# A state-space and MLP block on one core: the last four token tiles get a PSUM tile each, and the last is multiplied in two column halves

## The chip, the cores and the metric

The kernel runs on one core of a Trainium2 chip. The metric is the device time of one execution in microseconds (us), here as the median of a few runs. A profile is one execution recorded by the hardware profiler; its span goes from the first instruction to the last.

## The reference

A layer with two residual halves over 2048 tokens of width 512: a state-space convolution (S4), then an MLP. Layer norms go ahead of each; the MLP has a second one inside.

```python
def _B_ref(x, w1, b1, w2, b2):
    y = _layernorm(x, axis=-1)
    h = _gelu(jnp.einsum("bsd,df->bsf", y, w1) + b1)      # 512 -> 1376
    return jnp.einsum("bsf,fd->bsd", h, w2) + b2          # 1376 -> 512

x = A_u                                                    # (1, 2048, 512), bfloat16
h = x + _A_ref(_layernorm(x, axis=-1), ...)                # S4: y = irfft(rfft(u) * rfft(K)) + u * Dskip
h2 = h + _B_ref(_layernorm(h, axis=-1), B_w1, B_b1, B_w2, B_b2)
return h2
```

The change lies in the last product, `h @ w2`, its residual add and its stores.

## The kernel before

The whole kernel is written as a list of operations. `add(engine, cost, fn, r=, w=, new=)` puts one operation on the list with what it reads and writes; an estimated cost goes with it. `S.run` then plays the list through on a model of the engines and gives each engine its order: at every step the engine that could start first takes the ready operation with the lowest rank. The program is issued in that order, so a change of a cost or of a dependency can move instructions.

PSUM is cut into four slots of 128 x 1024 float32 values (`NSL = 4`). An object `Ps()` stands for one use of a slot; it takes a free slot at the operation that names it in `new`, and gives it back when all operations that read or write it are planned. Dependencies on PSUM are kept for the whole `Ps` object, not for its columns: an operation that writes any part of it comes after every earlier operation that reads any part. If the model sees TensorE without work for over 0.6 us, it puts in filler matmuls (`fill`, L1451) on a free slot.

The tokens are worked in four groups of 512: `mlp(0, 0)`, `mlp(0, 1)`, `mlp(1, 0)` and `mlp(1, 1)`, the last of them at the very end of the kernel. Each call makes, for 512 tokens:

- the first product, 11 slices of 128 hidden values (the last has 97 rows, 96 and a row of ones for the bias), 4 matmuls of 512 columns for each (L1341), and ScalarE's Gelu out of PSUM into `hT` (L1343);
- the second product, in two rounds (`jp`) of two token tiles (`z`) of 128 tokens. One `Ps` holds both tiles of a round, 512 columns each. A tile takes 11 matmuls of 128 x 512 (L1358), one for each slice of `hT` with its own weight load, in three operations of 4, 4 and 3;
- the residual add on VectorE (L1360), which reads the tile's 512 columns in PSUM and the residual in SBUF and writes a bfloat16 buffer `ot` (eight of these in turn);
- two stores of 64 rows x 512 columns, 64 KB each (L584), both issued by SyncE (`dma("SP", ...)`).

So the second tile of a round writes to a `Ps` that the first tile's add reads: its first matmul waits for that add. In the last call the order on TensorE is: tile 1 (11 matmuls), 4 matmuls of tile 3, tile 2 (11), the other 7 of tile 3, 3 filler matmuls, tile 4 (11). At the end of the program SyncE waits for every store and the engines meet at a barrier (L1491).

`not_[0]` counts the token tiles as they are listed, 1 to 16, four for each call.

Of the kernel before, what the change touches and what calls it, by code (L numbers as in the profile page):

```python
# [9 lines left out]
ACT = mybir.ActivationFunctionType  # L10
ALU = mybir.AluOpType
# [234 lines left out]
class Sched:  # L246
# [10 lines left out]
    def add(self, eng, cost, fn, r=(), w=(), new=(), lat=0.0, pr=None, byts=0, soft=(), softw=(), hv=None):  # L257
        o = Op()
        o.soft = sorted({self.wr[k] for x in soft for k in self.keys(x) if k in self.wr} | {i for x in softw for k in self.keys(x) for i in self.rd.get(k, ())})
        o.eng = eng if isinstance(eng, tuple) else (eng,)  # L260
        o.cost = cost if isinstance(cost, tuple) else (cost,)
        o.fn, o.lat, o.i, o.new, o.byts = fn, lat, len(self.ops), tuple(new), byts
        o.ni, o.act = 0, 0.0
        o.hv = int(o.eng[0] == "DVE") if hv is None else hv
        o.pr = self.pr if pr is None else pr
        o.key = "%g%s" % (o.pr, o.eng[0][0])
        o.pr = RANK.get(o.key, o.pr)
        deps = set()
        for x in r:
            for k in self.keys(x):  # L270
                p = self.wr.get(k)
                if p is not None:
                    deps.add(p)
        for x in w:
            for k in self.keys(x):
                p = self.wr.get(k)
                if p is not None:
                    deps.add(p)
                deps.update(self.rd.get(k, ()))
        for x in r:  # L280
            for k in self.keys(x):
                self.rd.setdefault(k, []).append(o.i)
        for x in w:
            for k in self.keys(x):
                self.wr[k] = o.i
                self.rd[k] = []
        o.deps = sorted(deps)
        o.ps = [x for x in list(r) + list(w) if isinstance(x, Ps)]
        self.ops.append(o)
        return o  # L290
# [143 lines left out]
def c_act(n, ptr=0):  # L434
    return 0.055 + n / 1200.0 + 0.09 * min(ptr, 1)


def c_dve(n, mode=1, psum=False):
    return (0.09 if n < 64 else 0.065) + (0.07 if psum and n > 700 else 0) + n / mode / 960.0
# [3 lines left out]
def kernel(ctx, tc, A_u, A_A_re, A_A_im, A_B_re, A_B_im, A_C_re, A_C_im, A_log_dt, A_Dskip,  # L443
           B_x, B_w1, B_b1, B_w2, B_b2, out):
    nc = tc.nc
    act, dve, gp = nc.scalar, nc.vector, nc.gpsimd
# [15 lines left out]
    pe = Pe()  # L462
# [9 lines left out]
    add = S.add  # L472

    def pst(p, dt=f32):
        a = slots[p.slot][:]
        return a if dt == f32 else a.bitcast(dt)
# [7 lines left out]
    def at(lo, dt, *shape):  # L484
        return V(ar, lo, dt, shape)
# [96 lines left out]
    def dma(q, out_fn, in_fn, byts, r, w, pr=None, soft=(), k=1.0):  # L582
        eng = {"SP": nc.sync, "ACT": nc.scalar, "POOL": nc.gpsimd}[q]
        add(q, 1.0 if q == "POOL" else 0.55, lambda e: eng.dma_start(out_fn(), in_fn()), r=r, w=w, byts=byts * k, pr=pr, soft=soft)  # L584
# [174 lines left out]
    def tr(nm):  # L759
        p = Ps()  # L760

        def fn(e):
            for d in range(4):
                pe.transpose(pst(p, bf16)[:, 128 * d:128 * d + 128], raw[nm].ap()[:, d, :], identb.ap())
        add("PE", 0.6, fn, r=[raw[nm], identb], w=[p], new=[p])
        return p, (lambda: nat(pst(p, bf16)[:, 0:512]))
# [3 lines left out]
    p, pa = tr("are")  # L770
# [22 lines left out]
    p = Ps()  # L793
# [41 lines left out]
    p, pa = tr("aim")  # L835
# [385 lines left out]
    NFC = 11  # L1221
    fsz = [P] * 10 + [97]
# [7 lines left out]
    hT = at(Kg[0].lo, bf16, NFC, 512)  # L1230
    w1s = [at(EA2.lo + 2752 * c, bf16, F) for c in range(4)]
    w2s = [at(IA2.lo + 1024 * fc, bf16, 512) for fc in range(11)]
# [3 lines left out]
    ov = out_dram.rearrange("(b q h j) d -> b h j q d", b=2, j=8, h=2)  # L1236
# [90 lines left out]
    not_ = [0]  # L1327

    def mlp(b, sb, ybuf, pr):
        S.pr = pr  # L1330
        for f0 in range(0, NFC, 2):
            p = Ps()
            for z in range(2):
                fc = f0 + z
                if fc >= NFC:
                    continue
                fs = min(P, F - fc * P)

                def fn(e, p=p, z=z, fc=fc, fs=fs):
                    for dc in range(4):  # L1340
                        pe.matmul(pst(p)[:fs, 512 * z:512 * z + 512], lhsT=w1s[dc].ap()[:, fc * P:fc * P + fs], rhs=ybuf.ap().rearrange("p (t c) k -> p c t k", c=4)[:, dc], start=(dc == 0), stop=(dc == 3))  # L1341
                add("PE", 0.87, fn, r=[ybuf] + w1s, w=[p], new=[p] if z == 0 else [])
                add("ACT", c_act(512, 1), lambda e, p=p, z=z, fc=fc, fs=fs: act.activation(hT.ap()[:fs, fc, :], pst(p)[:fs, 512 * z:512 * z + 512], ACT.Gelu_apprx_tanh, bias=b1_sb.ap()[:fs, fc:fc + 1], scale=1.0),  # L1343
                    r=[p, b1_sb, TBL], w=[hT[fc]])
        for jp in range(2):
            p = Ps()
            for z in range(2):
                t = 2 * jp + z
                j = 4 * sb + t
                hh = hs[8 * b + j]  # L1350
                ot = ots[not_[0] % 8]
                not_[0] += 1

                for part in ((0, 4), (4, 8), (8, 11)):
                    def fn(e, p=p, z=z, t=t, part=part):
                        for fc in range(*part):
                            fs = fsz[fc]
                            pe.matmul(pst(p)[:, 512 * z:512 * z + 512], lhsT=hT.ap()[:fs, fc, 128 * t:128 * t + 128], rhs=w2s[fc].ap()[:fs], start=(fc == 0), stop=(fc == NFC - 1))  # L1358
                    add("PE", 0.217 * (part[1] - part[0]), fn, r=[hT[part[0]:part[1]]] + w2s[part[0]:part[1]], w=[p], new=[p] if z == 0 and part[0] == 0 else [])
                add("DVE", c_dve(512, 1, True), lambda e, p=p, z=z, hh=hh, ot=ot: dve.tensor_tensor(ot.ap(), pst(p)[:, 512 * z:512 * z + 512], hh.ap(), ALU.add), r=[p, hh], w=[ot])  # L1360
                for h in range(2):
                    dma("SP", lambda j=j, h=h: ov[b, h, j], lambda ot=ot, h=h: ot.ap()[64 * h:64 * h + 64], 65536, [ot], [("out", b, j, h)])

# [61 lines left out]
    tail(0, 0, y2T[0], 30)  # L1427
    tail(0, 1, y2T[1], 31)
    mlp(0, 0, y2T[0], 70)
    xspec(1, Two(XB), 18.8, q_="SP")  # L1430
    for c in range(NCH):
        inverse(1, c, [(KFb[0][c], XBc[c]), (KFb[1][c], XR[c])], ZT1[c], 52 + 3 * c)
    load_x(1, 65)
    mlp(0, 1, y2T[1], 71)
    tail(1, 0, y2T[2], 66)
    tail(1, 1, y2T[0], 67)
    mlp(1, 0, y2T[2], 73)
    mlp(1, 1, y2T[0], 74)

# [56 lines left out]
```

## Time and profile before

| | |
|---|---|
| median of 3 runs (lowest, highest) | 271.92 us (271.52, 274.41) |
| the profiled execution, whole | 270.04 us |
| its span | 268.3 us |
| granted TensorE clock | 1.00 |
| TensorE busy | 233.6 us, 87% |
| VectorE busy | 186.6 us, 70% |
| ScalarE busy | 169.2 us, 63% |
| L1358, second product, 128 x 512 | 172 recorded matmuls, 380 ns each |
| L1360, residual add | 16, 691 ns each |
| stores of the output | 32 of 64 KB, 2.0 us from issue to landing |

In the profile's rows a line such as L1358 is a line of the kernel's file, `ps` is PSUM and `ar` the one large SBUF buffer in which all tiles lie. PE is TensorE, PEld its weight loads, DVE VectorE, ACT ScalarE and SP SyncE; a `q` behind the name means the engine's instruction queue, where DMAs are issued. Matmuls overlap: each lasts some 0.38 us by the record, while the next starts about 0.21 us after it.

### The profile page before, as it was taken

The page shows a single profiled execution, that of the slowest core. Times are in us where ns is not written, and L with a number is a line of the kernel's source. Part 1 is how long each engine was busy: PE and PEld are TensorE (multiplying, and loading weights), DVE is VectorE, ACT ScalarE, POOL GpSimd, SP SyncE. Part 2 cuts the span into 40 slices and gives each one's busy share as a digit, 9 for nine tenths or more (in the row PEclk, how much of TensorE's full clock was granted, in tenths as well). Part 3 has the DMA queues.
Part 4 walks back from the last instruction along what each step waited for, and adds up shares of the span by engine and source line. Part 5 has one row for each costly group of instructions (what it writes and reads, how often), then busy time and mean ns, then how long its engine had stood idle before and what let it go on. Part 6 is the DMA issues. An engine that isn't in the chain of part 4 may idle for free.

```text
span 268.3 us, 7345 instructions
## 1 busy us (share of the span) xinstructions
PE 233.6 (87%) x3038; PEld 132.4 (49%) x3058; DVE 186.6 (70%) x366; ACT 169.2 (63%) x202; POOL 59.3 (22%) x237
## 2 busy tenths in 40 slices
PE   7128788686889999999989999799999999999993
PEld 3015553343477656673667776454444444444441
DVE  3899999999999897576965986798447249031031
ACT  3798989898988598868962773457405504704700
POOL 8999923699600000000000000000000000000000
PEclk9999999999999999999999999999999999999999
DMA  6800100270755377979999999913411402411011
GB/s 139 312 1 1 42 20 20 64 216 0 169 149 161 101 220 246 363 220 306 299 288 270 235 231 204 212 24 57 78 42 39 78 20 59 81 32 47 0 33 48
DMA packets 45843, 34.36 MB, mean 128 GB/s; under 512 B 26129, under 2 KB 42226, under 8 KB 45810
## 3 DMA queue, kind: packets, MB, share of 16 engines
q1 hardware_dynamic: 45378, 33.50, 48.4%
q8 instruction: 24, 0.39, 0.6%
q10 hardware_dynamic: 432, 0.39, 0.5%
q14 instruction: 9, 0.07, 0.1%
HBM read 16.32 MB, written 10.49 MB: 100 GB/s over the span
## 4 chain that ended last, share of the span: by engine, by line
PE 61%; DVE 18%; ACT 6%; POOL 6%; issue 4%; DMA 2%; SPq 1%; DVEq 0%; ACTq 0%; POOLq 0%
PE ps L1358 14%; PE ps L1341 14%; PE ps L1209 7%; PE ps L971 4%; PE ps L1451 4%; ACT ar L572 4%; PE ps L1159 3%; PE ps L1046 3%; DVE ar L923 3%; DVE ar L634 2%; POOL ar L620 2%; ACT ar L1052 2%; PE ps L1287 2%; DMA AU_d<-ar 2%; PE ps L1125 2%
## 5 line engine op out<-in xcount | busy, mean ns | idle before, releaser
L572 ACT CAST ar<-ps 128x1024 bf16<-128x1024 f32 (+3 forms) x68 | 61.0, 938 | 28.8 <-PE ps L1209 17.3
L1343 ACT ACTIVATE ar<-ps,ar 128x512 bf16<-128x512 f32 (+1 forms) x44 | 29.8, 685 | 41.4 <-PE ps L1341 28.8
L574 DVE CAST ar<-ps 128x1024 bf16<-128x1024 f32 (+2 forms) x32 | 37.3, 1181 | 8.9 <-PE ps L971 3.4
L620 POOL TENSOR_SCALAR ar<-ar 128x128 bf16<-128x128 bf16 (+6 forms) x60 | 38.1, 656 | 6.8 <-ACT ar L641 6.6
L1358 PE MATMUL ps<-ar 128*128 128x512 bf16 (+1 forms) x172 | 39.1, 380 | 0.6 <-DVE ar L1360 0.4
L1341 PE MATMUL ps<-ar 128*128 128x512 bf16 (+1 forms) x176 | 38.6, 379 | 0.1
L1360 DVE TENSOR_TENSOR ar<-ps,ar 128x512 bf16<-128x512 f32 x16 | 11.1, 691 | 38.0 <-PE ps L1358 27.6
L1052 ACT ACTIVATE ar<-ps 128x1024 bf16<-128x1024 int16 x36 | 35.3, 1037 | 1.9 <-PE ps L1046 1.4
L1199 DVE TENSOR_TENSOR ar<-ar 128x1024 bf16<-128x1024 bf16 x48 | 30.1, 686 | 8.0 <-PE ps L1209 7.8
L1358 PEld LDWEIGHTS <-ar 128*128 128x128 bf16 (+1 forms) x176 | 16.8, 97 | 22.5 <-issue 3.1
L1341 PEld LDWEIGHTS <-ar 128*128 128x128 bf16 (+1 forms) x176 | 17.6, 100 | 20.7 <-issue 0.4
L1209 PE MATMUL ps<-ar 64*128 64x128 bf16 x768 | 23.7, 217 | 2.6 <-DVE ar L1295 1.4
L1046 PE MATMUL ps<-ar 128*32 128x256 f16 x560 | 22.2, 275 | 3.9 <-ACT ar L1052 2.7
L1209 PEld LDWEIGHTS <-ar 64*128 64x128 bf16 x768 | 21.6, 94 | 7.2 <-issue 5.0
L1451 PE MATMUL ps<-ar 128*128 128x512 bf16 (+1 forms) x77 | 20.7, 387 | 0.6 <-ACT ar L572 0.2
L1046 PEld LDWEIGHTS <-ar 128*32 128x32 f16 x560 | 13.6, 97 | 13.9 <-issue 13.7
L971 PE MATMUL ps<-ar 128*64 128x512 bf16 (+1 forms) x160 | 17.6, 342 | 0.6 <-ACT ar L572 0.3
L784 ACT ACTIVATE ar<-ar 128x1024 bf16<-128x1024 f32 x16 | 15.8, 1043 | 2.2 <-DVE ar L618 2.2
L1294 DVE TENSOR_TENSOR ar<-ps,ar 128x512 bf16<-128x512 f32 x12 | 7.8, 685 | 11.7 <-ACT ar L1343 11.1
L641 ACT ACTIVATE ar<-ar 128x512 f32<-128x512 f32 (+8 forms) x18 | 11.6, 675 | 5.5 <-DMA ar<-in_A_log_dt_dram 2.1
L1426 POOL MEMSET ar<- 1x512 bf16 x1 | 0.5, 519 | 65.1 <-DVE ar L574 65.1
L1072 DVE TENSOR_TENSOR ar<-ar 128x1024 bf16<-128x1024 bf16 x21 | 14.6, 713 | 0.4 <-ACT ar L1052 0.4
(99 smaller groups left out, 322.6 us busy)
## 6 DMA issues: line engine op xcount, KB each, us to landing
AU_d<-ar SPq DMA_DIRECT2D x16, 256.0 KB, 4.9
ar<-AU_d SPq DMA_DIRECT2D x8, 512.0 KB, 6.7
ar<-AK_d SPq DMA_DIRECT2D x8, 512.0 KB, 5.5
ar<-in_A_u_dram SPq DMA_DIRECT2D x4, 512.0 KB, 6.8
AK_d<-ar SPq DMA_DIRECT2D x2, 1024.0 KB, 6.5
ar<-in_A_u_dram SPq DMA_DIRECT2D x8, 256.0 KB, 7.7
AK_d<-ar SPq DMA_DIRECT2D x4, 512.0 KB, 7.9
out_dram<-ar SPq DMA_DIRECT2D x32, 64.0 KB, 2.0
```

Source lines behind the costliest of these rows:

```text
L572: act.copy(out_fn(), in_fn())
L574: dve.tensor_copy(out_fn(), in_fn())
L620: en.tensor_scalar(a, b, f(s1), f(s2), op0, op1)
L971: pe.matmul(pst(p)[64 * h:64 * h + 64, w * (k + r):w * (k + r) + w], lhsT=T.ap()[:, f, r, :], rhs=v[f:f + 1].ap()[:, 0, :], start=True, st ...
L1046: pe.matmul(pst(p)[32 * g:32 * g + 32, 256 * j:256 * j + 256], lhsT=W2[DELTAS.index(d)].ap(), rhs=S2[g].ap()[:, ch0:ch0 + 256], start=Fals ...
L1052: add("ACT", c_act(1024), lambda e, p=p, sc=sc, cs=cs: act.activation(swo(sc[cs]) if hf and kind == "B" else sc[cs].ap().rearrange("p a b ...
L1199: dve.tensor_tensor(o, a, b_[:, :, ::-1, :] if sw else b_, ALU.mult)
L1209: pe.matmul(pst(p)[:, 512 * h + 128 * k:512 * h + 128 * k + 128], lhsT=q.ap()[rows, 2 * k + r, :], rhs=TP[w].ap()[rows, f0 // 2 + k, :], s ...
L1341: pe.matmul(pst(p)[:fs, 512 * z:512 * z + 512], lhsT=w1s[dc].ap()[:, fc * P:fc * P + fs], rhs=ybuf.ap().rearrange("p (t c) k -> p c t k", ...
L1343: add("ACT", c_act(512, 1), lambda e, p=p, z=z, fc=fc, fs=fs: act.activation(hT.ap()[:fs, fc, :], pst(p)[:fs, 512 * z:512 * z + 512], ACT. ...
L1358: pe.matmul(pst(p)[:, 512 * z:512 * z + 512], lhsT=hT.ap()[:fs, fc, 128 * t:128 * t + 128], rhs=w2s[fc].ap()[:fs], start=(fc == 0), stop=( ...
L1451: pe.matmul(slots[z][:, 0:512], lhsT=w, rhs=x, start=True, stop=True)
```

## The change

The tiles 13 to 16, the four of the last call, are marked with `fin`. Each of them gets a `Ps` of its own. The last tile is made in two halves of 256 columns, each with its own `Ps`, 11 matmuls, an add and two stores of 64 rows x 256 columns; of these, the stores of the lower 64 rows go through ScalarE's queue. The cost of a matmul in the list is now by column (0.000424 x 512 = 0.217, as before). For the first twelve tiles the operations are the same.

```diff
-                for part in ((0, 4), (4, 8), (8, 11)):
-                    def fn(e, p=p, z=z, t=t, part=part):
-                        ...
-                            pe.matmul(pst(p)[:, 512 * z:512 * z + 512], ..., rhs=w2s[fc].ap()[:fs], ...)
-                    add("PE", 0.217 * (part[1] - part[0]), fn, ..., w=[p], new=[p] if z == 0 and part[0] == 0 else [])
-                add("DVE", c_dve(512, 1, True), ... dve.tensor_tensor(ot.ap(), pst(p)[:, 512 * z:512 * z + 512], hh.ap(), ALU.add), r=[p, hh], w=[ot])
-                for h in range(2):
-                    dma("SP", lambda j=j, h=h: ov[b, h, j], ... ot.ap()[64 * h:64 * h + 64], 65536, [ot], [("out", b, j, h)])
+                fin = not_[0] > 12
+                cols = ((0, 256), (256, 512)) if not_[0] == 16 else ((0, 512),)
+                for c0, c1 in cols:
+                    if fin and z + c0 > 0:
+                        p = Ps()
+                    for part in ((0, 4), (4, 8), (8, 11)):
+                        def fn(e, p=p, z=z, t=t, part=part, c0=c0, c1=c1):
+                            ...
+                                pe.matmul(pst(p)[:, 512 * z + c0:512 * z + c1], ..., rhs=w2s[fc].ap()[:fs, c0:c1], ...)
+                        add("PE", 0.000424 * (c1 - c0) * (part[1] - part[0]), fn, ..., w=[p], new=[p] if part[0] == 0 and (fin or z == 0) else [])
+                    add("DVE", c_dve(c1 - c0, 1, True), ... dve.tensor_tensor(ot.ap()[:, c0:c1], pst(p)[:, 512 * z + c0:512 * z + c1], hh.ap()[:, c0:c1], ALU.add), r=[p, hh], w=[ot[c0:c1]])
+                    for h in range(2):
+                        dma("ACT" if h and len(cols) == 2 else "SP", lambda ...: ov[b, h, j][:, c0:c1], ... ot.ap()[64 * h:64 * h + 64, c0:c1], 128 * (c1 - c0), [ot[c0:c1]], [("out", b, j, h, c0)])
```

More of the change, by code (lines that the diff above doesn't have):

```diff
@@ L1352, in mlp @@
                 not_[0] += 1
-                for part in ((0, 4), (4, 8), (8, 11)):
-                    def fn(e, p=p, z=z, t=t, part=part):
[L1356 to L1360, printed above, removed]
-                for h in range(2):
-                    dma("SP", lambda j=j, h=h: ov[b, h, j], lambda ot=ot, h=h: ot.ap()[64 * h:64 * h + 64], 65536, [ot], [("out", b, j, h)])
+                fin = not_[0] > 12
[5 more added lines that the diff above has]
+                        def fn(e, p=p, z=z, t=t, part=part, c0=c0, c1=c1):
+                            for fc in range(*part):
+                                fs = fsz[fc]
+                                pe.matmul(pst(p)[:, 512 * z + c0:512 * z + c1], lhsT=hT.ap()[:fs, fc, 128 * t:128 * t + 128], rhs=w2s[fc].ap()[:fs, c0:c1], start=(fc == 0), stop=(fc == NFC - 1))
+                        add("PE", 0.000424 * (c1 - c0) * (part[1] - part[0]), fn, r=[hT[part[0]:part[1]]] + w2s[part[0]:part[1]], w=[p], new=[p] if part[0] == 0 and (fin or z == 0) else [])
+                    add("DVE", c_dve(c1 - c0, 1, True), lambda e, p=p, z=z, hh=hh, ot=ot, c0=c0, c1=c1: dve.tensor_tensor(ot.ap()[:, c0:c1], pst(p)[:, 512 * z + c0:512 * z + c1], hh.ap()[:, c0:c1], ALU.add), r=[p, hh], w=[ot[c0:c1]])
+                    for h in range(2):
+                        dma("ACT" if h and len(cols) == 2 else "SP", lambda j=j, h=h, c0=c0, c1=c1: ov[b, h, j][:, c0:c1], lambda ot=ot, h=h, c0=c0, c1=c1: ot.ap()[64 * h:64 * h + 64, c0:c1], 128 * (c1 - c0), [ot[c0:c1]], [("out", b, j, h, c0)])
     S.pr = 8
```

## The prediction

> **What bounds the kernel now.** I read the page first, for the span and the stores, then the chain of work that ended last over the final 30 us, then the timeline of the last 10 us, and last the rows that give prices for shapes which the end does not have yet. The core works at a granted clock of 1.00 throughout, and the change touches only what is issued after 253.28 us, so only the end needs to be read.
>
> The chain of work that ended last, in order of time (start, length, what):
>
> ```profile
> 253.28 7.23 PE ps L1358 x32
> 260.51 0.04 DVEq L1360
> 260.55 0.04 issue
> 260.59 0.70 DVE ar L1360
> 261.29 0.04 issue
> 261.33 2.55 PE ps L1358 x11
> 263.88 0.02 issue
> 263.91 0.69 DVE ar L1360
> ```
>
> TensorE multiplies three of the last four tiles in one run (33 matmuls, one without a record) and ends at 260.51. Then it waits: the VectorE add of the third tile, 0.70 us, stands between it and the fourth tile's 11 matmuls, because both tiles share one PSUM tile and the kernel's list of dependencies knows only the whole tile. The fourth tile ends at 263.88, its add at 264.60. The timeline shows what TensorE does in the gap, and what follows the last add:
>
> ```profile
> 260.33 0.81 PE L1451 MATMUL ps<-ar 128*128 128x512 bf16 x3
> ...
> 264.63 1.10 SPq L584 DMA_DIRECT2D out_dram<-ar  x2
> ```
>
> The three L1451 matmuls are filler that keeps the clock up; their first start, 260.33, is where the fourth tile could have started. After the last add SyncE issues two stores one behind the other (1.10 us together; the second starts at 265.1). The list of SyncE's waits and the view of the output tensor give the rest:
>
> ```profile
> SPq L1491 <- DMA out_dram<-ar: 1.5, 1, 1.5
> ...
> DMA to landing us min/median/max: 1.9/2.0/3.5
> ```
>
> A store lands about 2.0 us after its issue, so the second one lands near 267.2, where the 1.5 us wait of the program's end (from 265.8) ends too. 1.1 us of closing semaphores follow, to 268.3. So the last 8 us are one serial chain: wait for an add, 11 matmuls, an add, two issues, a landing, the close.
>
> **The change, part by part.** The instruction order of the changed kernel is the same as before up to the eighth matmul row of the second tile; nothing earlier moves on any engine.
>
> *Own PSUM tiles.* The four tiles go to four different slots, the fourth's second half to a fifth, which is the first tile's slot again. Before, two matmuls of L1358 waited for VectorE: the second tile's first (hidden behind four matmuls of the third) and the fourth's. Now only the very last group waits, for the first tile's add, which ends at 255.70 + 0.69 = 256.39, some 5 us earlier. The three slots that are newly entered were last read by ScalarE, whose last reading ends at 253.33 + 0.69 = 254.02. So TensorE runs on without a stop, the filler is gone, and the fourth tile starts at 260.33 in place of 261.33.
>
> *Two column halves.* 11 matmuls of 512 columns become 22 of 256, with 22 weight loads in place of 11. The end of the kernel has no such matmul, but its beginning has, with weights of the same 128x128:
>
> ```profile
> 24.60 1.04 PE L1004 MATMUL ps<-ar 128*128 128x256 f16 x8
> ...
> L1004 PEld LDWEIGHTS <-ar x80: 95/98/153, 21.9 to 39.2; 128*128 128x128 f16 x80
> L1004 PE MATMUL ps<-ar x80: 268/273/422, 22.3 to 39.3; 128*128 128x256 f16 x80
> ```
>
> Eight take 1.04 us, of which the last one's own duration is 0.273, so one follows the other after (1.04 - 0.273) / 7 = 0.110 us, and the weight load of 0.098 lies beside it. 22 of them take 21 x 0.110 + 0.273 = 2.58 us, against 2.55 for the 11 wide ones. TensorE therefore ends at 260.33 + 2.58 = 262.91 in place of 263.88: 0.97 us gained, all of it from the lost wait. The bound on the other side is that the loads are not hidden at all (22 x 0.097 = 2.13 us more); I take the row, since it is the same shape.
>
> *Half an add at the end.* The first half's add runs while TensorE does the second half: it can start near 261.7 and is over by 262.2, ahead of the last at 262.94. For the price of 256 columns out of PSUM I have another line's pair of shapes beside the add's own row:
>
> ```profile
> L1360 DVE TENSOR_TENSOR ar<-ps,ar 128x512 bf16<-128x512 f32 x16 | 11.1, 691 | 38.0 <-PE ps L1358 27.6 <-issue 7.7 <-DMA out_dram<-ar 2.6
> ...
> L629 DVE TENSOR_TENSOR ar<-ps,ar 128x512 f32<-128x512 bf16 x4 | 2.5, 682 | 0.0
> ...
> L629 DVE TENSOR_TENSOR ar<-ps,ar 128x256 f32<-128x256 bf16 x2 | 0.8, 420 | 3.5 <-PE ps L764 3.5
> ```
>
> Half the columns cost 682 - 420 = 262 ns less, so the last add takes 691 - 262 = 429 ns and 0.26 us is gained. The add ends at 262.94 + 0.43 = 263.37.
>
> *Stores.* Two stores of 64 KB become four of 32 KB; the first pair is issued from about 262.25 and SyncE is free again by 262.8 or so (it is busy with the third tile's stores from 261.3 to 262.4), before the last pair at 263.40. ScalarE has nothing else to do after 254.02, so nothing queues behind its two issues. The last pair is now issued side by side by SyncE and ScalarE, so the second issue at 264.63 + 0.5 is no longer behind the first: up to 0.5 us. What two queues do to each other is seen only in the first microseconds, in loads:
>
> ```profile
> 1.66 0.42 ACTq L584 DMA_DIRECT2D ar<-in_A_B_re_dram  x1
> 1.67 0.44 SPq L584 DMA_DIRECT2D ar<-in_A_C_im_dram  x1
> ...
> ar<-in_A_B_re_dram ACTq DMA_DIRECT2D x1, 128.0 KB, 4.1
> ...
> ar<-in_A_C_im_dram SPq DMA_DIRECT2D x1, 128.0 KB, 4.3
> ```
>
> Issued 0.01 us apart, neither issue longer than alone, they land 0.2 us apart. So of the 0.5 I count 0.3, with bounds of 0 (the pair costs as much as one behind the other) and 0.6 (half the bytes also land a little sooner). The last landing is then near 263.40 + 2.0 + 0.2 = 265.6 in place of 267.2.
>
> The Trainium skill speaks against this part: DMA: Bandwidth & Descriptors, section Rules for kernel authors, says of two transfers to disjoint partition halves not to bother, since both spread over the same 16 DMA engines and serialise whichever engine issued them; its section on issuing engines grants two queues only the issue time. The 0.2 us between the landings of the two loads above agrees with the shared engines; by that rule the gain of this part is the 0.3 taken here, not 0.5. A stricter rule is a rival below.
>
> **Sum.** 0.97 + 0.26 + 0.3 = 1.53 us, every term on the one chain, and the closing 1.1 us unchanged. The profiled execution takes 270.04 us, its span 268.3 and 1.7 around it; the changed one should show a span near 266.8 and 268.5 in all. The three runs shown have their median at 271.92, 1.9 above the profiled one; taking the same 1.53 from the median gives 270.4, or 0.6% less.
>
> **Rivals.**
> 1. *The second queue saves nothing.* The pair's second store starts its work only when the first is through with its issue, as it does now on one queue. Then the stores give 0 and the gain is 1.23: 270.7. For it: now each issue takes about 0.5 and the second store lands that much later. Against it: the loads at 1.66 and 1.67. Perfetto Trace Analysis, section DMA Instruction — HWDGE, in the Trainium skill says that the descriptor block is shared by the issuing sequencers and locked for exclusive use, which would do just this; the side-by-side issues of 0.42 and 0.44 us do not show a lock of such length.
> 2. *Weight loads come out from behind the narrow matmuls* (the other side). A load of 0.097 us beside a matmul step of 0.110 leaves 0.013 to spare; if each pair runs one after the other, the last tile takes 22 x 0.097 = 2.13 us more than I count, and the result is 271.92 - 1.53 + 2.13 = 272.5. It decides for slower from a step of 0.110 + 1.53 / 22 = 0.18 us. Against it: L1004 does the same at 0.110.
> 3. *A late last store.* One store of the first of the last four tiles took 3.5 us to land where the others took 2.0. If the last one, on a queue unused since the first 2 us, comes out like that, 1.5 of the 1.53 is lost: 271.9. Against it: that landing lies next to an instruction fetch near 257.5, and ScalarE's first loads, on a queue just as unused, land like SyncE's.
> 4. *The change does not lift the wait*, because a slot is still held or filler stays in. Then only 0.26 + 0.3 remains: 271.4. The issue order excludes nearly all of it: the last group's wait is for an add that is long done.
>
> **How the numbers follow.** The forecast has 0.76, the rivals 0.1, 0.05, 0.06 and 0.03. The likeliest time is 270.4. The mechanism alone gives 270.1 (0.6 for the stores) to 270.7. A time as measured also carries the runs' own scatter: the three of before lie from 271.52 to 274.41, and the profiled one at 270.04, so a median of a few can stand 1 us off in either direction. The range goes from 269.1 (forecast, 1.3 low) to 271.9 (rivals 3 and 4, or the forecast 1.5 high). About 1% is what a measurement of this kernel can tell from no change, 2.7 us, and no row allows a gain of that size: the bounds add up to 0.97 + 0.26 + 0.6 = 1.83. Faster by over 1% is thus the forecast and scatter together, a quarter; slower by over 1% needs rival 2 or 3 and scatter, 0.05; the rest, 0.70, lies within 1%.
>
> **What would show it.** Right: the chain near its end reads L1358 without a VectorE piece between matmuls from 253.28 to about 262.9; no L1451 after 241.0 us; two adds of 0.43 us, the last starting near 262.94; SyncE and ScalarE issues within 0.05 us of each other near 263.4; a span near 266.8. Wrong in the first step: a VectorE piece still between L1358's groups. Wrong in the second: 22 narrow matmuls that take much over 2.6 us. Wrong in the third: last landing more than 2.4 us after its issue. Wrong altogether: a difference that begins before 253 us.

## The result and the profile after

The changed kernel takes 268.80 us (median of 6 runs, 268.11 to 270.64) against 271.72 for the kernel before (median of 6, 271.25 to 274.41): ratio 0.9886, 95% interval 0.9838 to 0.9935. Two more comparisons of the same two kernels, with 12 runs of the changed one in each, gave 0.9953 (0.9926 to 0.9981) and 0.9930 (0.9890 to 0.9970), at medians of 269.85 and 270.00 us. The medians are over all runs; the ratios leave out runs that lie over 1.5% above the fastest of their kernel. All three intervals lie below 1, so the changed kernel is faster, by about 0.6%; the first figure of 1.1% did not come back. The forecast of 270.4 us stands near the two later medians, and its range of 269.1 to 271.9 misses the first one by 0.3.

The profiled execution of the changed kernel has a span of 268.9 us, 0.6 longer than the one shown of before, so spans must not be compared here. The end of the kernel can be. The chain of work that ended last, in order of time (start, length, what), reads now:

```profile
245.97 9.50 PE ps L1341 x44
255.47 9.56 PE ps L1363 x55
265.02 0.02 issue
265.05 0.42 DVE ar L1365
```

There is no VectorE piece between the matmuls any more: all 55 of the last four tiles (33 wide and 22 narrow) are one run. The groups by form in the last 14 us (count | busy us, mean ns of one | idle before):

```profile
L1363 PEld LDWEIGHTS <-ar 128*128 128x128 bf16 x50 | 4.9, 98 | 4.0
L1363 PE MATMUL ps<-ar 128*128 128x256 bf16 x20 | 2.5, 272 | 0.0
...
L1365 DVE TENSOR_TENSOR ar<-ps,ar 128x256 bf16<-128x256 f32 x2 | 0.8, 424 | 1.2 <-PE ps L1363 1.2
```

The narrow matmuls are as L1004's were, without idle time, and the half add takes 424 ns. The timeline of the last microseconds, then the DMA view with the size and the time from issue to landing:

```profile
263.41 2.55 SPq L584 DMA_DIRECT2D out_dram<-ar  x4
...
264.36 1.65 ACTq L584 DMA_DIRECT2D out_dram<-ar  x2
```

```profile
out_dram<-ar ACTq DMA_DIRECT2D x2, 32.0 KB, 2.1
out_dram<-ar SPq DMA_DIRECT2D x2, 32.0 KB, 2.0
```

The last pair, in the timeline from 265.2 us on:

```profile
265.50 0.47 SPq L584 DMA_DIRECT2D out_dram<-ar  x1
265.50 0.50 ACTq L584 DMA_DIRECT2D out_dram<-ar  x1
```

It is issued side by side, at 265.50 by both engines. The two stores land 2.08 us (SyncE) and 2.26 us (ScalarE) later; in the kernel before, the first of the last pair took 1.92.

To set kernels side by side I count from the first add of the last four tiles, ahead of which the kernel before and the changed one issue the same instructions in the same order. The stretch from there to the end of the span is called the tail below; the first expectations count theirs from the first recorded matmul of the last product instead, 2.4 to 2.6 us earlier. All times in us from the first add, two profiles of the kernel before, three of the changed one, one of each other kernel:

| kernel | TensorE ends | last add ends | last store lands | span ends |
|---|---|---|---|---|
| before (two profiles) | 8.17 | 8.90 | 11.48, 11.49 | 12.57, 12.56 |
| changed | 7.07 | 7.54 | 9.74 to 9.82 | 10.85 to 10.92 |
| own tiles alone | 7.04 | 7.77 | 10.36 | 11.43 |
| own tiles, two queues | 7.04 | 7.77 | 10.00 | 11.02 |
| own tiles, halves, one queue | 7.07 | 7.54 | 10.44 | 11.48 |
| halves and two queues, shared tile | 8.88 | 9.34 | 11.46 | 12.56 |

The end is shorter by 12.57 - 10.92 = 1.65 to 12.56 - 10.85 = 1.71 us, 0.6% of 271. It repeats within 0.1 us, while the first add stands anywhere from 255.41 to 259.68 us in the nine profiles of the table. Most of the gain comes from the own tiles: they alone bring 1.14 us of the tail (12.57 to 11.43), the second queue 0.41 more (11.02), and the halves the last 0.10 to 0.17.

### The profile page after: what moved, and what is told of

The parts are those of the page before. It is cut to its first block, busy times and chain, and to the rows that moved or that the text cites. A ratio compares the mean times of both kernels' runs of the same rounds, so it can differ in the third digit from the quotient of the medians.

```text
span 268.9 us, 7389 instructions
## 1 busy us (share of the span) xinstructions
PE 236.0 (88%) x3066; PEld 133.6 (50%) x3066; DVE 186.8 (69%) x367; ACT 169.2 (63%) x202; POOL 58.4 (22%) x237
## 4 chain that ended last, share of the span: by engine, by line
PE 49%; DVE 18%; DMA 14%; POOL 6%; ACT 6%; issue 4%; SPq 2%; DVEq 0%; ACTq 0%; POOLq 0%
PE ps L1363 14%; PE ps L1341 14%; DMA AK_d<-ar 6%; DMA ar<-in_B_w_dram 4%; ACT ar L572 3%; DVE ar L923 3%; PE ps L1046 3%; PE ps L971 3%; DVE ar L634 2%; POOL ar L620 2%; ACT ar L1052 2%; DMA AU_d<-ar 2%; PE ps L1125 2%; PE ps L1287 2%; SPq L584 2%
## 5 line engine op out<-in xcount | busy, mean ns | idle before, releaser
L574 DVE CAST ar<-ps 128x1024 bf16<-128x1024 f32 (+2 forms) x32 | 37.3, 1181 | 10.7 <-PE ps L971 4.5
L1363 PE MATMUL ps<-ar 128*128 128x512 bf16 (+3 forms) x187 | 39.4, 367 | 0.2 <-DVE ar L1365 0.2
L620 POOL TENSOR_SCALAR ar<-ar 128x128 bf16<-128x128 bf16 (+6 forms) x60 | 37.3, 643 | 6.8 <-ACT ar L641 6.6
L1341 PE MATMUL ps<-ar 128*128 128x512 bf16 (+1 forms) x176 | 38.6, 379 | 0.1
L1365 DVE TENSOR_TENSOR ar<-ps,ar 128x512 bf16<-128x512 f32 (+1 forms) x17 | 11.2, 660 | 36.4 <-PE ps L1363 28.7
L1363 PEld LDWEIGHTS <-ar 128*128 128x128 bf16 (+1 forms) x187 | 17.9, 98 | 21.2 <-issue 2.4
L1341 PEld LDWEIGHTS <-ar 128*128 128x128 bf16 (+1 forms) x176 | 17.6, 100 | 20.6 <-issue 0.4
L1456 PE MATMUL ps<-ar 128*128 128x512 bf16 (+1 forms) x83 | 20.4, 386 | 0.0
L1294 DVE TENSOR_TENSOR ar<-ps,ar 128x512 bf16<-128x512 f32 x12 | 7.8, 683 | 11.7 <-ACT ar L1343 11.1
```

The lines of the kernel that those rows point to most:

```text
L574: dve.tensor_copy(out_fn(), in_fn())
L620: en.tensor_scalar(a, b, f(s1), f(s2), op0, op1)
L1363: pe.matmul(pst(p)[:, 512 * z + c0:512 * z + c1], lhsT=hT.ap()[:fs, fc, 128 * t:128 * t + 128], rhs=w2s[fc].ap()[:fs, c0:c1], start=(fc == ...
L1456: pe.matmul(slots[z][:, 0:512], lhsT=w, rhs=x, start=True, stop=True)
```

## The experiments

Two theories were set against each other. By the tail theory the change is worth what the end of the trace shows and no more. By the whole-kernel theory it also speeds up something ahead, which would make up the 2.9 us of the first comparison.

**The two kernels once more.** No edit.

> The kernel before against itself, to see the scatter. Both theories expect a ratio of 1.000, with an interval that shows how far a ratio can stray by chance. Tail theory (the change is worth only what its traces show after the first L1358 matmul of the last round, 15.0 us before and 13.4 after): the stretch ahead of that matmul, 253.3 us in the first profile, comes out different by 1 us or more here, and the tail again 15.0 within 0.1. Whole-kernel theory (the change also speeds up something ahead of the tail, by another 1.3 us): the stretch ahead of the tail stays at the upper end, near 254.5 to 255.5.

Measured: ratio 1.0013 (0.9976 to 1.0051), 12 runs from 269.43 to 275.9 us. The tail is 12.56 (14.98 as the expectation counts it); the first add stands at 257.55 where the first profile had it at 255.70.

> The changed kernel once more. Tail theory: tail 13.4 us again, the time 1.6 us (0.6%) under the kernel before, ratio 0.994, the first comparison's 0.9886 having been scatter of the stretch ahead. Whole-kernel theory: ratio 0.989 again, 2.9 us.

Measured: ratio 0.9953 (0.9926 to 0.9981), tail 10.85.

> The changed kernel a third time, since its first two comparisons gave 0.9886 and 0.9953. Tail theory (1.65 to 1.72 us of 271, all of it after the first add of the last four tiles): a ratio near 0.994, with a profile whose stretch ahead of that add is the kernel before's, 255.4 to 257.9 us, as the run has it. Whole-kernel theory: 0.989.

Measured: ratio 0.9930 (0.9890 to 0.9970), tail 10.86, first add at 257.81. What follows: the tail theory holds as far as these runs can tell. 0.994, the tail's share, lies inside both repeats' intervals and just outside the first comparison's (0.9935 at most); 0.989 lies outside the first repeat's and just on the edge of the second's. The prediction named a difference that begins before 253 us as the sign of being altogether wrong. There is one: the first add stands at 257.81 to 257.94 in the three profiles of the changed kernel, 2.1 to 2.2 us later than in the first profile of the kernel before. But the kernel before, run again, has it at 257.55, and the kernel with own tiles alone at 255.41, so this difference comes and goes without the change. It also arises early: from the third call's first add to the last call's it is 20.14 us in all nine profiles of the table.

Where the scatter ahead of the tail comes from is partly to be seen. The busy time of the engines PE, PEld, DVE, ACT and POOL (GpSimd) from 48 to 52 us, in the first profile of the kernel before and then in that of the same kernel run again (the figure behind POOL's is the granted clock, then the DMA share and GB/s):

```profile
48.00:52.00 4.00, 3.05 (x40) 1.34 (x39) 3.90 (x8) 3.20 (x5) 2.58 (x5) 1.00 0.13 29
```

```profile
48.00:52.00 4.00, 3.69 (x24) 1.17 (x23) 3.90 (x8) 2.85 (x5) 2.60 (x5) 0.61 0.08 20
```

In some executions the clock falls to half for 3.4 us here, in others not, with the same instructions, and in the changed kernel too (0.60 in its first profile). In the second of these profiles ScalarE's work is 0.33 us late after it. That is not all: the third profile of the changed kernel has the full clock throughout and is 2 us behind the first profile of the kernel before all the same, from about 157 us on. There the list of waits from 130 to 180 us has lines that the first profile of the kernel before does not have in that stretch:

```profile
PEld L971 <- DMA ar<-AK_d: 1.5, 2, 1.0
...
PE ps L971 <- DMA ar<-AK_d: 1.0, 2, 0.8
```

TensorE waits for loads, in a stretch where the DMA engines are busy nearly all the time. The second profile of the kernel before has both waits too, 0.7 and 0.5 us, and is 1.83 us late from 157 us on, so they come without the change too. Why these loads come later in one execution than in another is not shown.

**Own tiles alone.**

```diff
-                cols = ((0, 256), (256, 512)) if not_[0] == 16 else ((0, 512),)
+                cols = ((0, 512),)
```

> Only the own PSUM tiles: each of the last four tiles has a use of PSUM of its own, the last is multiplied whole, and all stores go by SyncE. Tail theory: TensorE runs through, the tail is 15.0 - 0.97 = 14.0 us, two stores issued one behind the other at the end, ratio 0.996. Whole-kernel theory: if the unexplained part comes with the own tiles, ratio near 0.992 with a tail of 14.0.

Measured: ratio 0.9957 (0.9931 to 0.9983), tail 11.43 from the first add, 13.85 from the first recorded matmul: 1.14 us less than before where 0.97 was expected, or 1.00 without the 0.03 for narrow matmuls, which this kernel does not have. The chain of this kernel shows where the other 0.14 come from:

```profile
252.99 9.47 PE ps L1363 x43
262.46 0.02 issue
262.48 0.69 DVE ar L1365
```

With (9.47 - 0.38) / 42 the step is 0.216 us. In the kernel before, the run of 32 recorded matmuls takes (7.23 - 0.38) / 31 = 0.221: its 31 steps hold 0.14 us too much. In the trace that is one step of 0.35 between two matmuls, where the second tile waits for the first tile's add. I had called this wait hidden behind four matmuls of the third tile; they cover all but 0.14 us of it.

**Own tiles and halves, one queue.**

```diff
-                        dma("ACT" if h and len(cols) == 2 else "SP", ...)
+                        dma("SP", ...)
```

> The whole change but for the queue: own tiles and column halves, all stores by SyncE. Tail theory: last add 0.26 us shorter than in the kernel with own tiles alone, the last store's issue 0.5 us behind the one before it, so a tail of 13.4 + 0.3 = 13.7 us, between 13.4 (a second queue is worth nothing) and 14.0 (worth all of the issue time); ratio 0.995. Whole-kernel theory: if the second queue brings the unexplained part, the ratio is at 0.995 here while the full change stays at 0.989.

Measured: ratio 1.0001 (0.9968 to 1.0034), tail 11.48 from the first add. Counted as the expectation counts it, from the first recorded matmul, it is 13.9 against 13.85 with own tiles alone, so the expected 13.7 was missed: next to the whole change (10.85 to 10.92) the second queue is worth 0.56 to 0.63 us here, twice the 0.3 that was counted. The ratio was missed too: its interval leaves out the expected 0.995 and does not show the 1.1 us that the trace shows gained, though the medians do in part (270.05 against 270.85). Whether scatter of the size just shown is all of that, one profile cannot tell. The tail alone says that halving brings nothing without the second queue, and the timeline shows what eats the shorter add:

```profile
261.12 3.66 SPq L584 DMA_DIRECT2D out_dram<-ar  x6
261.61 0.42 DVE L1365 TENSOR_TENSOR ar<-ps,ar 128x256 bf16<-128x256 f32 x1 [0.52 <-PE ps L1363]
262.76 0.42 DVE L1365 TENSOR_TENSOR ar<-ps,ar 128x256 bf16<-128x256 f32 x1 [0.72 <-PE ps L1363]
```

SyncE issues six stores without a stop, 0.6 us each. The last add ends at 263.18, but the first store of the last half is issued only at 263.60, 0.42 after it, and the second 0.60 later. The add ends 0.23 us earlier than in the kernel with own tiles alone, the last landing is 0.08 later.

**Own tiles and the second queue, whole last tile.**

```diff
-                cols = ((0, 256), (256, 512)) if not_[0] == 16 else ((0, 512),)
+                cols = ((0, 512),)
...
-                        dma("ACT" if h and len(cols) == 2 else "SP", ...)
+                        dma("ACT" if h and not_[0] == 16 else "SP", ...)
```

> Own PSUM tiles, the last tile multiplied and added whole, its two 64 KB stores issued by SyncE and ScalarE side by side. Read from the end of the trace, counted from the first add of the last four tiles to the end of the span (12.57 us in the kernel before, 11.43 with own tiles alone, 10.85 to 10.92 with the whole change). Tail theory: the second queue takes 0.3 us off the own tiles, 11.1 us. If the second queue is worth nothing without the halves: 11.4. If it is worth all of the 0.5 us between two issues: 10.9.

Measured: tail 11.02, 0.41 less than own tiles alone (ratio 0.9934, 0.9885 to 0.9982), so between the expected 11.1 and the 10.9 of a queue that is worth all of the issue time. The timeline has both issues at the same moment, and the DMA view has the landings:

```profile
264.44 0.47 SPq L584 DMA_DIRECT2D out_dram<-ar  x1
264.45 0.55 ACTq L584 DMA_DIRECT2D out_dram<-ar  x1
```

```profile
out_dram<-ar SPq DMA_DIRECT2D x1, 64.0 KB, 1.9
out_dram<-ar ACTq DMA_DIRECT2D x1, 64.0 KB, 2.2
```

To 0.01 us, the stores land 1.93 (SyncE) and 2.20 us (ScalarE) after their issues, where one queue had them 1.92 and 2.04 after issues 0.52 apart. The second issue comes 0.51 us sooner after the add; of this, 0.16 comes back as a later landing, and 0.35 is gained there. The rest of the 0.41 lies in the close.

**Halves and two queues without own tiles.**

```diff
-                fin = not_[0] > 12
+                fin = False
...
-                        add("PE", ..., new=[p] if part[0] == 0 and (fin or z == 0) else [])
+                        add("PE", ..., new=[p] if part[0] == 0 and z == 0 and c0 == 0 else [])
```

> Column halves of the last tile and the second queue, but PSUM as in the kernel before: two token tiles share one PSUM tile, and so do the two halves. Tail theory: the waits stay, and a second one comes in, as the second half's first matmul waits for the first half's add: drain 0.17, add 0.43 and 0.06 of signalling, 0.66 us. The last add is 0.27 us shorter and the stores 0.3 us: 12.57 + 0.66 - 0.57 + 0.04 for narrow matmuls = 12.7 us from the first add to the end, no better than before. If the halves and the queue are worth something by themselves, it is 12.0.

Measured: tail 12.56, the same as the kernel before; ratio 1.0003 (0.9976 to 1.0030). Its chain has two waits:

```profile
264.53 0.04 issue
264.57 0.70 DVE ar L1365
265.28 0.04 issue
265.32 1.38 PE ps L1363 x11
266.70 0.02 issue
266.72 0.44 DVE ar L1365
267.16 0.04 issue
267.20 1.38 PE ps L1363 x11
```

The second half starts 0.50 us after the first has ended, so TensorE ends 0.71 us later than in the kernel before (8.88 against 8.17). What shorter add and second queue bring (0.73 against 0.46 us for the add, then 2.58 against 2.12 to the landing) is just eaten. The parts of the change do not add up. On own tiles the halves cost 0.05 us with one queue (11.43 to 11.48) and bring 0.10 to 0.17 with two; without own tiles, halves and second queue together bring nothing. The second queue alone on shared tiles was not run.

**Further the same way.** Own tiles for the last eight token tiles, with the halves and queues as in the change:

```diff
-                fin = not_[0] > 12
+                fin = not_[0] > 8
```

> The whole change, with own PSUM tiles for the last eight token tiles in place of four (the last two of the four calls). Tail theory: the wait of 0.82 us that the chain shows at 240.5 us in the kernel before goes too, with the 0.16 us that the second tile waits; the end is as in the changed kernel (10.85 to 10.92 from the first add), and from the last call's first L1341 matmul nothing else changes. 1.0 to 1.1 us under the changed kernel, ratio to the kernel before 0.991. Rival: the call's next product waits for something else (its layer norm, transposes), and nothing is gained over the changed kernel, 0.995.

Measured: 267.85 us, the lowest median of all kernels here, and ratio 0.9888 (0.9855 to 0.9921). This interval overlaps two of the changed kernel's three, so the trace has to show the gain. The tail is 10.82, as in the changed kernel, and the chain has nothing but TensorE over the last two calls:

```profile
224.31 9.50 PE ps L1341 x44
233.81 9.51 PE ps L1363 x44
243.32 9.50 PE ps L1341 x44
252.82 9.56 PE ps L1363 x55
```

In the kernel before, the chain through the third call's second product was

```profile
233.09 0.05 issue
...
240.45 0.70 DVE ar L1360
...
243.73 1.30 PE ps L1341 x6
```

It took from 233.09 (the first matmul has no record) to the next L1341 at 243.73, 10.64 us; now it takes 9.51. The third call's first add stood 20.14 us ahead of the last call's, now 19.01. Both ways 1.13 us are gained, as much as in the last call, where 1.0 to 1.1 was expected.

> The whole change, with own PSUM tiles for all sixteen token tiles. In the first two calls of the kernel before the chain shows no VectorE piece between L1358's matmuls: TensorE has 8 matmuls of L1287 to do between the third and the fourth tile, which cover the wait. Tail theory: nothing more to gain than with eight, ratio 0.990, and perhaps a loss, as PSUM's four slots are now taken by single tiles where other work wants them. Rival: each call gains the 1.1 us that the third and the fourth gained, two more: 0.981.

The edit is `fin = True`. Measured: ratio 0.9894 (0.9860 to 0.9928), no more than with eight. In the kernel before, the chain through the second call's products was

```profile
211.89 0.99 PE ps L1287 x8
...
213.25 6.87 PE ps L1358 x31
220.12 0.99 PE ps L1287 x8
221.11 2.48 PE ps L1358 x11
223.59 9.50 PE ps L1341 x44
```

and with sixteen own tiles it is

```profile
212.98 0.99 PE ps L1287 x8
213.97 9.62 PE ps L1363 x44
223.58 1.85 PE ps L1287 x16
225.44 1.40 PE ps L1456 x6
226.84 9.50 PE ps L1341 x44
```

L1287's matmuls stood where the wait would have been, and covered it. With own tiles the second eight of each call no longer stand there: sixteen of them come behind the second call's 44, and then six filler matmuls (L1456), 1.40 us, which the kernel before does not have there. The next L1341 follows the filler without a gap, so the trace does not show how early it could have started, nor what the planner saw missing. From the first call's L1341 to the third's it takes 226.84 - 183.22 = 43.62 us in place of 223.59 - 181.04 = 42.55, so 1.07 are lost in the first two calls, and the 1.13 of the third are taken back. The ratio is too coarse to show this loss. The same wait that costs 1.1 us in the last two calls costs nothing where TensorE has other work.

**A smaller last piece.** With eight own tiles, the last tile split into 384 and 128 columns.

```diff
-                cols = ((0, 256), (256, 512)) if not_[0] == 16 else ((0, 512),)
+                cols = ((0, 384), (384, 512)) if not_[0] == 16 else ((0, 512),)
```

> As the kernel with eight own tiles, but the last tile split into 384 and 128 columns. The last add is of 128 columns, 0.13 us shorter (0.29 by the step of 0.262 us for 256 columns), and each of the last stores moves 16 KB in rows of 256 bytes. Tail theory: 10.85 - 0.13 = 10.7 to 10.8 us from the first add to the end. Rival: rows under 512 bytes land later, and the end is at 10.9 us or above.

Measured: tail 11.68, 0.86 more than with two halves (10.82), so the forecast of 10.7 to 10.8 was missed; ratio 0.9939 (0.9903 to 0.9975). The last add does take 293 ns and ends 0.13 earlier. The stores lose it again:

```profile
out_dram<-ar SPq DMA_DIRECT2D x1, 48.0 KB, 1.9
out_dram<-ar ACTq DMA_DIRECT2D x1, 48.0 KB, 2.1
out_dram<-ar SPq DMA_DIRECT2D x1, 16.0 KB, 2.7
out_dram<-ar ACTq DMA_DIRECT2D x1, 16.0 KB, 2.5
```

Two things happen. The last pair is issued 0.29 (SyncE) and 0.66 us (ScalarE) after the last add, as the two queues have been at the 384-column stores until 0.20 and 0.28 after it; what holds ScalarE for 0.38 more the trace does not tell. And the 16 KB stores then take 2.5 to 2.7 us to land where 32 KB took 2.0 to 2.2. The Trainium skill, DMA: Bandwidth & Descriptors, Specifications, gives 512 bytes as the least transfer for full line rate. The later landing of 256-byte rows agrees with that, but these stores also follow closely on larger ones, and the two causes were not parted.

## Why the prediction was right or wrong, point by point

- *What bounds the end*: right. The chain of the changed kernel, and each kernel that took one link out of it, show the same links.
- *TensorE's term, 0.97 us*: the mechanism was right, the size too small. Measured 8.17 - 7.07 = 1.10. This is the one term of the sum that was mis-sized: the second tile's wait was put at nothing because four matmuls of the third tile stand in it, but they last 4 x 0.216 = 0.86 us and the wait, like that of the fourth tile, some 1.00, so 0.14 stood out. The narrow matmuls cost 0.03 as expected.
- *The last add, 0.26 us*: right. From TensorE's end to the add's end it is now 0.47 in place of 0.73. What the term leaves out is that the shorter add is worth something only with two queues, as the experiments show.
- *The stores, 0.3 us, between 0 and 0.6*: right, 2.58 to 2.20 or 2.29 from the add's end to the landing. The rule of the Trainium skill that I set against it (DMA: Bandwidth & Descriptors, Rules for kernel authors) agrees in what it says of shared engines, 0.16 us by the kernel with the whole last tile, but its advice not to bother does not fit the end of a kernel, where the other 0.35 us of issue time are on the path.
- *The sum, 1.53 us*: 1.65 to 1.71 in the trace. Rivals 1, 2 and 4 fell with the lines shown. Perfetto Trace Analysis, section DMA Instruction — HWDGE, in the Trainium skill speaks of a lock; two issues begun in the same moment took 0.47 and 0.50 us, so no lock as long as an issue is seen. Rival 3 did not occur in the changed kernel.
- *How the numbers follow*: this step failed. I let a median of a few runs stand 1 us off, and put the low end of the range 1.3 under the forecast. The measured 268.80 lies 1.6 under it. Of this, 0.2 is the start of the count: the median of the kernel before is 271.72 with six runs, where the three shown had 271.92. Some 0.15 is the sum, through the wait priced at nothing. The rest, 1.25, is more than the 1 us allowed, and no trace shows it as work of the change: the same kernel's two longer medians, 269.85 and 270.00, lie 1.05 and 1.2 above the first. What made those six runs fast stays open. That the scatter is larger than 1 us could have been seen from the profile shown: its execution was 1.5 us below the fastest of the three runs, with nothing in the kernel to account for it. The two longer comparisons found what was forecast, a gain under 1%; the first one is the reading over 1% to which I had given a quarter.

## What to carry to other kernels

A dependency that is kept for a whole buffer makes a wait between two users of its halves; look in the chain for a short piece of a second engine between two runs of the first, and give each user its own buffer where no other work fills the gap, for only there is it worth anything. At the end of a kernel every link is serial, also the issue of a store, so a shorter last piece pays only as long as the queues are free when it is done. A change at the end of a kernel is measured better by the time from a common instruction to the end of the trace (0.1 us of scatter here) than by the whole time (several us).

## What the runs showed of the hardware that I had not expected

- Two stores issued in the same moment by SyncE and ScalarE land 0.17 to 0.30 us apart, 1.8 to 2.3 us after the issue, where one queue needs 0.52 us more for the second issue.
- On one queue, stores of 32 KB are no cheaper than those of 64 KB: issues stand 0.60 to 0.68 us apart when four follow each other (0.52 between a pair of 64 KB), and each lands 1.9 us after its issue.
- The granted clock fell to half for 3.4 us near 49 us in some executions and not in others of one and the same instruction order (0.61 against 1.00 from 48 to 52 us in two profiles of the kernel before).
